# A new order of issue and new buffers for an adaLN, Hedgehog attention and MLP kernel on one core

## The chip, the cores and the metric

The kernel runs on one core of a Trainium2 chip. The metric is the device time of one execution in microseconds, as a median of runs. A profiled execution of the same kernel gives a page of figures and a trace; its span is a little shorter than the measured time. TensorE is PE in the profile (its weight loads PEld), VectorE is DVE, ScalarE is ACT, GpSimd is POOL, and SyncE is SP, whose queue issues nearly all the DMA transfers.

## The reference

One batch, S = 2048 tokens, D = 512, 32 heads of 16, a hidden width of F = 1376, all in fp32. Cut to what matters:

```python
mod = (silu(c) @ w_mod).reshape(1, 6, 1, -1)          # sa, ca, ga, sb, cb, gb
h = layernorm(x) * (1 + ca) + sa
q, k, v = heads(h @ wqkv)
pq, pk = q @ w_phi, k @ w_phi                         # per head, 16 x 16
phi_q = concat([softmax(pq), softmax(-pq)])           # 32 features per head
phi_k = concat([softmax(pk), softmax(-pk)])
kv = sum_s phi_k^T v ;  z = sum_s phi_k               # over all tokens, per head
o = (phi_q @ kv) / (phi_q . z + 1e-6)
x = x + ga * (o @ wo)
h = layernorm(x) * (1 + cb) + sb
x = x + gb * (gelu_tanh(h @ w1 + b1) @ w2 + b2)
```

The sum over all tokens in kv and z divides the work: nothing behind it can be finished before all keys and values are done.

## The kernel before

The work is tiled into eight blocks of 256 tokens (two tiles of 128). Products of full precision are made of three matmuls (`mm3`, line 287): each operand is split into a high and a low part, and high·high, high·low and low·high are added. A projection of one tile is thus a group of 12 matmuls of 128 rows by 512 columns; the rows "x12", "x24" of the chain are such groups.

The program has twelve parts. Part 0 loads, folds w_phi into the key and query weights (tiles `fold`), makes the modulation vectors and the layernorm of block 0 (`hT` is a block transposed). Parts 1 to 6 project keys, values and some queries (`pk`, `pv`, `pq` are PSUM banks), make the exponentials `ek`, and add up kv (`pkv`, a run of small matmuls in plain fp32). Part 7 closes the sums: `kvT` is copied by ScalarE, two small products `zp` and `kvp` follow, and `zb` is z spread over the partitions. It then does the attention of blocks 0 and 1, lays out w1 (`w1`, w2 as `w2a` and `w2b`), and starts on the MLP. Parts 8 to 11 run the MLP for pairs of blocks (`pg` is the hidden layer before and after the bias, `g` its GELU split in two, `py` the second product), with the attention of the later blocks threaded between.

Attention of a block (`attn_a`, line 742): with `eq` the exponentials of the queries of a tile, `ez` = eq·zb, `dz` its sum per head and sign, `den` the denominators, `rd` their reciprocal, `rcq` the factors of the rows, and last eq·rcq. In the two first blocks one of the two `ez` and one of the two last products go to VectorE, the rest to GpSimd; from block 2 on GpSimd has them all. Blocks 0 and 1 are then turned by TensorE (`qp`, `attn_t`, line 798, copies `qT`); in later blocks VectorE turns 32x32 pieces into `eb`, eight stores (`et_dram`) bring them to DRAM, and two loads bring them back as `eT` (`attn_ea`, line 779). `po` (`attn_o`, line 816) is the product with kv, copied into `oT` by ScalarE and VectorE, and `pw` the product with wo. `x1` is the residual; a second layernorm gives `h2`, `yp` its transposition by TensorE, and `yT` the result. Queries that are projected early are parked in DRAM: `qs` is the copy, `pq_dram` the store, `pq` the load.

The order is written out by hand, as data. `Held` and `Later` (lines 210 to 243) do not issue an operation but record it, in a queue by part and by "item.letter", where the letter is that of the engine (p, a, v, g, s for TensorE, ScalarE, VectorE, GpSimd, SyncE). `issue` then takes them out in the order of the twelve strings of `ISSUE` (line 87), one string for each part; a + or − in front of a name takes the operation from a later or an earlier part. One global sequence is thus cut into one queue for each engine, and each engine works through its own in order. All operations therefore have the line 218 in the profile. A framework sets the semaphores that the data and the buffers need.

Buffers are data too: `SLOTS` (line 46) has for each tag a string with one character for each allocation, which `slot` (line 258) reads. There are 19 large buffers ("buf"), 8 PSUM banks ("bank"), and two or three buffers for the small tags. Which earlier tile an allocation waits for follows from these characters.

## Time and profile before

| what | value |
|---|---|
| time, median of 3 runs | 467.59 us (467.13 to 468.8) |
| span of the profiled execution | 466.6 us, so 1.0 below the median |
| granted clock of TensorE | full speed in every slice |
| busy: PE, DVE, ACT, POOL | 458.5, 317.1, 234.6, 279.7 us |
| DMA moved | 68.05 MB, 146 GB/s on the mean |

The page gives each engine's busy time, its share of the span and its number of instructions, then the chain of work that ended last. A row of the chain or of a timeline is: start in us, length in us, engine, tile and line, and how many instructions; in square brackets the idle time before it and what ended that. A row of the waits is: who waited for whom, us in total, how often, the longest. In rows of groups, what stands after the bar is busy us, mean ns of one, and idle time before.

### The profile page before, as it was taken

The numbers are of one execution on the slowest core, as the hardware profiler recorded it, in microseconds if no ns is written. First come the engines' busy times: TensorE is split into PE (matmuls) and PEld (weight loads), VectorE is DVE, ScalarE is ACT, GpSimd is POOL, SyncE is SP. The second block draws the span as 40 slices with busy tenths as digits, with TensorE's granted clock in tenths as the row PEclk, the third lists the DMA queues.
The fourth block names the chain that finished last, engine by engine and source line by source line (L and its number), as shares of the span: only waits on it lengthen the run. The fifth ranks groups of instructions, "written<-read, shape, count | busy, mean of one in ns | idle before, by whom it ended". The sixth has DMA issues, their size and how long they took to land.

```text
span 466.6 us, 8536 instructions
## 1 busy us (share of the span) xinstructions
PE 458.5 (98%) x3297; PEld 372.3 (80%) x3297; DVE 317.1 (68%) x612; ACT 234.6 (50%) x381; POOL 279.7 (60%) x233
## 2 busy tenths in 40 slices
PE   8999999999999999999999999999999999999996
PEld 5887888888878878978787878787788788788884
DVE  5999999989938599389797579896484472221113
ACT  4757866767440827848537743176133234422221
POOL 2369587999799998989899684756721020300000
PEclk9999999999999999999999999999999999999999
DMA  8998738492372664836837728077445504000003
GB/s 311 382 311 301 195 84 276 95 269 55 100 257 95 189 209 90 244 104 139 224 135 160 225 53 241 1 130 178 143 90 136 122 14 93 15 30 1 1 1 135
DMA packets 83673, 68.05 MB, mean 146 GB/s; under 512 B 54688, under 2 KB 70960, under 8 KB 83376
## 3 DMA queue, kind: packets, MB, share of 16 engines
q1 hardware_dynamic: 83632, 67.50, 50.9%
q8 instruction: 26, 0.43, 0.4%
q14 instruction: 15, 0.12, 0.1%
HBM read 44.94 MB, written 22.55 MB: 145 GB/s over the span
## 4 chain that ended last, share of the span: by engine, by line
PE 85%; DMA 5%; DVE 4%; POOL 2%; issue 1%; ACT 1%; SPq 0%; DVEq 0%; POOLq 0%; ACTq 0%
PE py L218 25%; PE pg L218 24%; PE pv L218 8%; PE pk L218 8%; PE pw L218 8%; PE pq L218 7%; PE pkv L218 2%; DMA wm<-in_wmodT 2%; PE po L218 1%; DVE pw L218 1%; DMA eT<-et_dram 1%; DMA wms<-in_wmodT 1%; DMA xt<-in_x 1%; PE qp L218 1%; POOL w2a L218 1%
## 5 line engine op out<-in xcount | busy, mean ns | idle before, releaser
L218 PE MATMUL pg<-yT,w 128*128 128x512 f32 (+1 forms) x528 | 115.3, 371 | 0.6 <-DVE yT L218 0.3
L218 PEld LDWEIGHTS pg<-yT,w 128*128 128x128 f32 x528 | 92.8, 188 | 18.5 <-DVE yT L218 0.5
L218 ACT ACTIVATE pg<-pg,blob 128x512 f32<-128x512 f32 x44 | 29.1, 662 | 100.6 <-PE pg L218 100.4
L218 PE MATMUL py<-w2a,g 128*128 128x512 f32 x288 | 70.7, 391 | 0.0
L218 DVE TENSOR_TENSOR g<-pg,g 128x512 fp32r<-128x512 f32 x40 | 27.2, 680 | 61.7 <-ACT g L218 61.7
L218 PEld LDWEIGHTS py<-w2a,g 128*128 128x128 f32 x288 | 53.6, 188 | 12.6 <-issue 1.6
L218 PE MATMUL pk<-wk,hT 128*128 128x512 f32 x192 | 46.2, 392 | 0.8 <-ACT hT L218 0.7
L218 PE MATMUL py<-w2b,g 128*128 128x512 f32 x192 | 46.9, 391 | 0.0
L218 PE MATMUL pv<-wvh,hT 128*128 128x512 f32 x192 | 45.9, 392 | 0.0
L218 PE MATMUL pw<-wo,oT 128*128 128x512 f32 x192 | 45.4, 390 | 0.0
L218 PE MATMUL pq<-wq,hT 128*128 128x512 f32 x192 | 45.3, 391 | 0.0
L218 PEld LDWEIGHTS pk<-wk,hT 128*128 128x128 f32 x192 | 35.6, 188 | 9.1 <-ACT hT L218 1.1
L218 PEld LDWEIGHTS py<-w2b,g 128*128 128x128 f32 x192 | 35.9, 188 | 8.1 <-issue 0.7
L218 PEld LDWEIGHTS pw<-wo,oT 128*128 128x128 f32 x192 | 35.9, 188 | 7.8 <-issue 0.4
L218 PEld LDWEIGHTS pv<-wvh,hT 128*128 128x128 f32 x192 | 35.7, 188 | 7.5
L218 PEld LDWEIGHTS pq<-wq,hT 128*128 128x128 f32 x192 | 35.8, 188 | 7.3
L218 POOL TENSOR_TENSOR ez<-eq,zb 128x1024 f32<-128x1024 f32 x15 | 36.8, 2469 | 5.5 <-ACT last L218 3.0
L218 POOL TENSOR_TENSOR yT<-yf,yT 128x256 fp32r<-128x256 f32 x24 | 17.2, 742 | 35.1 <-ACT yT L218 35.0
L218 POOL TENSOR_TENSOR ek<-ek,rck 128x1024 f32<-128x1024 f32 x16 | 30.8, 1939 | 4.5 <-DVE rck L218 2.3
L218 POOL TENSOR_TENSOR eq<-eq,rcq 128x1024 f32<-128x1024 f32 x15 | 28.9, 1937 | 0.3
L218 ACT ACTIVATE g<-pg 128x512 fp32r<-128x512 f32 x40 | 24.0, 599 | 9.5 <-PE pg L218 4.4
L218 DVE TENSOR_REDUCE smq<-eq 128x64 f32<-128x1024 f32 x16 | 19.2, 1207 | 6.8 <-ACT eq L218 6.8
(153 smaller groups left out, 783.4 us busy)
## 6 DMA issues: line engine op xcount, KB each, us to landing
et_dram<-eb SPq DMA_DIRECT2D x48, 128.0 KB, 2.9
eT<-et_dram SPq DMA_DIRECT2D x12, 512.0 KB, 5.1
xt<-in_x SPq DMA_DIRECT2D x8, 512.0 KB, 6.1
wms<-in_wmodT SPq DMA_DIRECT2D x8, 512.0 KB, 5.9
x<-in_x SPq DMA_DIRECT2D x8, 512.0 KB, 5.2
out<-x SPq DMA_DIRECT2D x15, 256.0 KB, 2.5
nt_dram<-nb SPq DMA_DIRECT2D x28, 128.0 KB, 3.4
hd<-nt_dram SPq DMA_DIRECT2D x7, 512.0 KB, 5.5
```

What stands on the lines that cost most here:

```text
L218: return lambda *a, **k: self.later.hold(self.letter, lambda: f(*a, **k))
```

## The change

The operations stay the same, in kind and number; only the strings of `SLOTS` and `ISSUE` are others. That changes the order on all five engines, and which tiles share a buffer. The loads of ScalarE's function table, which the framework sets where the function changes, go from 16 to 12 by the new order. One row in each of the two tables, the rest is of the same kind:

```diff
 SLOTS = {
     "buf":
-    "e93cf0idhabf4g55a2h17e4i27ce25986gi96f88af4a115357h8gbbf584dec522e4g0bai8761904137ecd23b5bh77df6ae2i"
+    "21638bca4938165777cd2aadbic0357e91b8a566ih449254975e1ee816dfd239917i83fdc5ha9654g632bbh0ebi2681bgfe7"
...
 ISSUE = [
...
-q2.p a1.g a0.v +a0.v q0.p a0.v +a0.g a1.v a1.g a0.v q2.p q2.a -v0.v a0.g a1.v a0.g q0.p a0.g a0.v a1.g a1.g a0.g
+a1.v q2.p q0.p a0.g q0.p a0.g a0.g a0.v --bg.a +a0.a +a0.v +a0.g a1.g a1.g a1.g +a0.a q2.a a1.v q1.p a0.g a0.v q4.a
```

GpSimd's queue in part 7, from the denominators of block 0 to the last product of block 1 (`den_401`, `rcq_228`, `eq_391` are of block 0; `dz_415`, `den_432`, `rcq_262`, `eq_406`, `eq_407` of block 1; `ez_522`, `ez_523` of block 2). Before:

```order
L218 TENSOR_TENSOR den_401<-den_401,deps_109 128x64
L218 TENSOR_TENSOR dz_415<-dz_415,rcq_262 128x128
L218 TENSOR_TENSOR den_432<-dz_415 128x64
L218 TENSOR_TENSOR rcq_228<-rcq_228,rd_402 128x128
L218 TENSOR_TENSOR den_432<-den_432,deps_109 128x64
L218 TENSOR_TENSOR eq_391<-eq_391,rcq_228 128x1024
L218 TENSOR_TENSOR rcq_262<-rcq_262,rd_433 128x128
L218 TENSOR_TENSOR eq_406<-eq_406,rcq_262 128x1024
L218 TENSOR_TENSOR eq_407<-eq_407,rcq_262 128x1024
L218 TENSOR_TENSOR ez_522<-eq_514,zb_116 128x1024
```

Now:

```order
L218 TENSOR_TENSOR den_401<-den_401,deps_109 128x64
L218 TENSOR_TENSOR ez_522<-eq_514,zb_116 128x1024
L218 TENSOR_TENSOR dz_415<-dz_415,rcq_262 128x128
L218 TENSOR_TENSOR den_432<-dz_415 128x64
L218 TENSOR_TENSOR den_432<-den_432,deps_109 128x64
L218 TENSOR_TENSOR rcq_228<-rcq_228,rd_402 128x128
L218 TENSOR_TENSOR eq_391<-eq_391,rcq_228 128x1024
L218 TENSOR_TENSOR rcq_262<-rcq_262,rd_433 128x128
L218 TENSOR_TENSOR ez_523<-eq_515,zb_116 128x1024
L218 TENSOR_TENSOR eq_406<-eq_406,rcq_262 128x1024
L218 TENSOR_TENSOR eq_407<-eq_407,rcq_262 128x1024
```

The two multiplications of block 2 moved ahead of what the blocks 0 and 1 still need; and the last quarter of the exponentials of block 2 (eq from mxq and pq, 128x512), which stood between the second and the third ez of the blocks 0 and 1, moved ahead of all three. VectorE's part of the same work, ez_400 and eq_390 of block 0, stays in its place between them.

SyncE's queue at the transposes of block 2 (`et_dram_100`, its loads `eT`; `pq_dram_75` holds the parked queries of block 4, tile pq_620 is their load; the numbers here are those of the tiles in DRAM). Before:

```order
L218 DMA et_dram_100<-eb 32x16x64 x8
L218 DMA pq_dram_75<-qs 128x1024
L218 DMA eT<-et_dram_100 128x4x256
L218 DMA w1s<-in_w 128x4x128
L218 DMA ws<-in_w 128x1024
L218 DMA eT<-et_dram_100 128x4x256
L218 DMA pq<-pq_dram_75 128x1024
L218 DMA x_530<-in_x 128x2x512
```

Now:

```order
L218 DMA pq_dram_75<-qs 128x1024
L218 DMA pq<-pq_dram_75 128x1024
L218 DMA et_dram_100<-eb 32x16x64 x8
L218 DMA eT<-et_dram_100 128x4x256 x2
L218 DMA x_530<-in_x 128x2x512
```

The store and the load of the parked queries went ahead of the eight stores; two weight loads that stood between the loads of eT moved elsewhere.

The same queue at the transposes of block 5 (`et_dram_103`; `x_696` is the second load of x for block 5). Before:

```order
L218 DMA out<-x_451 128x512 x2
L218 DMA et_dram_103<-eb 32x16x64 x8
L218 DMA pq<-pq_dram_78 128x1024
L218 DMA x_696<-in_x 128x2x512
L218 DMA eT<-et_dram_103 128x4x256 x2
```

Now:

```order
L218 DMA out<-x_451 128x512 x2
L218 DMA et_dram_103<-eb 32x16x64
L218 DMA x_696<-in_x 128x2x512
L218 DMA et_dram_103<-eb 32x16x64 x7
L218 DMA eT<-et_dram_103 128x4x256 x2
```

The load of x moved from behind the eight stores to behind the first. Its buffer is also another: by the new string it is one from which TensorE still reads a hidden tile g in the second product of an earlier pair of blocks.

Elsewhere: the first x load stands ahead of the load of the constants; the first query projection ahead of two pieces of the key projection; the small matmuls of `pkv` run in nine runs, not six; a query projection stands between the last of them and `zp`; one stage of `yp` stands ahead of a query projection, not behind it.

## The prediction

> **What bounds the kernel now.** I read the page's busy shares first, then the waits of TensorE, then the chain of waits, and last the timelines of the places where the order changes.

> ```profile
> PE 458.5 (98%) x3297; PEld 372.3 (80%) x3297; DVE 317.1 (68%) x612; ACT 234.6 (50%) x381; POOL 279.7 (60%) x233
> PE 85%; DMA 5%; DVE 4%; POOL 2%; issue 1%; ACT 1%; SPq 0%; DVEq 0%; POOLq 0%; ACTq 0%
> ```

> TensorE is busy for 98% of the span and has 85% of the chain; no other engine passes 68%. The change neither adds nor removes a matmul, so it can only win or lose the little time in which TensorE waits. That time stands in its waits (total us, times, longest):

> ```profile
> PE fold L218 <- DMA k<-in_wkT: 0.9, 1, 0.9
> PE pk L218 <- ACT hT L218: 0.7, 1, 0.7
> PE zp L218 <- ACT kvT L218: 0.6, 1, 0.6
> PE pg L218 <- DVE yT L218: 0.3, 1, 0.3
> PE pg L218 <- ACT yT L218: 0.3, 1, 0.3
> PE po L218 <- DMA eT<-et_dram: 0.2, 1, 0.2
> PE pk L218 <- POOL hT L218: 0.2, 1, 0.2
> ```

> These are 3.2 us in all, 0.7% of the span: an upper bound for what better order can take away, beside some startup time before the first dense matmul. A loss has no such bound, since each new wait on TensorE is time in full. So I look for the places where the new order gives an operand later than TensorE asks for it. The chain shows the rhythm around the end of the k/v stage:

> ```profile
> 97.85 1.84 PE pkv L218 x142
> 99.69 2.95 PE pv L218 x12
> ...
> 133.35 1.79 PE pkv L218 x116
> ...
> 135.66 1.99 PE zp L218 x8
> ...
> 137.87 16.36 PE pq L218 x72
> 154.24 1.75 PE qp L218 x16
> 155.98 2.73 PE pq L218 x12
> 158.71 1.02 PE po L218 x32
> ```

> Twelve matmuls of 512 columns take 16.36/6 = 2.73 us; I count the distance between two points of TensorE's order in these units.

> **The sum, part by part.** All terms are against the profiled span of 466.6 us; the median of the runs, 467.59, is 1.0 above it, which I add at the end.

> *Startup.* The first x load now goes out ahead of the constants, and the first query projection ahead of two pieces of the key projection. The two pk waits above (0.7 and 0.2) may shrink, or the later of two half blocks comes in late by as much: −0.2, bounds −0.9 and +0.9, the sum of the same rows either way.

> *Entries into pkv.* After a run of pkv the next 12 matmuls took 2.95 and not 2.73, so each entry costs 0.22. The change cuts the pkv work into nine runs where there were six: +0.7, bounds +0.4 and +0.9 (some runs are shorter).

> *Other waits of the k/v stage.* One v projection now stands 0.6 us of work behind the copy that frees its bank; others have over 2 us. +0.2, bounds 0 and +1.5 (two such copies at the 0.7 of the pk row above).

> *kvT.* A query projection (2.73) now stands between the last pkv and the z matmuls, which covers the 0.6 of the zp row: −0.6. The bounds are −0.6 and 0.

> *The first two attention blocks: the largest term.* Here GpSimd and VectorE multiply 128x1024 tiles, and they get in each other's way:

> ```profile
> 138.61 4.78 POOL L218 TENSOR_TENSOR ez<-eq,zb 128x1024 f32<-128x1024 f32 x2
> 143.32 1.09 POOL L218 TENSOR_TENSOR eq<-mxq,pq 128x512 f32<-128x512 f32 x1
> 144.35 3.41 POOL L218 TENSOR_TENSOR ez<-eq,zb 128x1024 f32<-128x1024 f32 x1
> 147.83 0.46 POOL L218 TENSOR_TENSOR dz<-dz,rcq 128x128 f32<-128x128 f32 x1
> 148.37 0.29 POOL L218 TENSOR_TENSOR den<-dz 128x64 f32<-128x64 f32 x1
> ...
> 149.88 0.43 POOL L218 TENSOR_TENSOR rcq<-rcq,rd 128x128 f32<-128x128 f32 x1
> ...
> 150.52 1.94 POOL L218 TENSOR_TENSOR eq<-eq,rcq 128x1024 f32<-128x1024 f32 x1
> 152.41 1.42 POOL L218 TENSOR_TENSOR rcq<-rcq,rd 128x128 f32<-128x128 f32 x1
> ```

> ```profile
> 143.33 2.16 DVE L218 TENSOR_TENSOR ez<-eq,zb 128x1024 f32<-128x1024 f32 x1
> ...
> 151.06 2.48 DVE L218 TENSOR_TENSOR eq<-eq,rcq 128x1024 f32<-128x1024 f32 x1
> ```

> ```profile
> L218 DVE TENSOR_TENSOR wvh<-wv_s,wvh 128x1024 fp32r<-128x1024 f32 x1 | 1.2, 1208 | 0.0
> ```

> The same size takes VectorE 1.21 alone. Its ez took 2.16 and ended at 145.49, 1.08 behind the end of GpSimd's eq (144.41); its eq took 2.48 and ended at 153.54, 1.08 behind the end of GpSimd's (152.46). GpSimd's next ez took 3.41 instead of 4.78/2 = 2.39, its rcq 1.42 instead of 0.43. The one waits for the end of the other. [...]

> Let E be the end of zp_397 and Z the start of GpSimd's first ez. Before, Z was 138.61 and E 137.65 (135.66+1.99). Now the last pkv, which GpSimd's work ahead of it waits for, ends a query projection earlier, so GpSimd stands ready, and I take 0.76, what the copy into zb needs; the 1.09 of eq that stood between the ez is ahead of them. The two ez of GpSimd end at Z+4.8. VectorE's ez_400, ready at Z+3.6, waits for that and ends at 5.85; GpSimd's ez_422, begun at 4.8, is held as long and ends at 8.1. Then come dz and den (1.2) and, new here, ez_522 (2.39): 11.7. The second block's dz and den take to 12.8, rcq_228 to 13.25, eq_391 (1.94) to 15.2. VectorE's eq_390 is held until then and ends at 16.25. TensorE asks for it after 72 matmuls: E+16.36 = Z+15.6. Wait: 0.7. Before, it was ready at 153.54 for 154.24, so a margin of 0.7 turns into a wait. Next on GpSimd: rcq_262, held by eq_390 until 16.5, the second new one, ez_523, to 18.9, eq_406 to 20.85, eq_407 to 22.8. TensorE, begun on qp at 16.3, wants eq_407 after 1.75+2.73+1.02 = 5.5, at 21.8: wait 0.9. And VectorE's rd_525, which needs GpSimd's den_524 behind eq_407, stands ahead of the copy oT1_419 that the first pw group needs: 0.25. Sum +1.85, bounds +0.2 (no holding, below) and +2.8 (the held ones at 1.42−0.43 more).

> *yT.* One transposition stage (yp_479) is ahead of a query projection: it covers the two yT waits (−0.6) but its h2 is due 2.7 us sooner (+0.6). Net 0, bounds −0.6 and +0.6.

> *Transposes of block 2.* In SyncE's queue the load of pq_620, which waits for the landing of its own store, now stands ahead of the eight stores of et:

> ```profile
> 183.27 5.14 SPq L218 DMA_DIRECT2D et_dram<-eb  x8
> 188.51 0.48 SPq L218 DMA_DIRECT2D pq_dram<-qs  x1
> ```

> ```profile
> 193.29 6.65 DMA eT<-et_dram
> ```

> ```profile
> 184.93 0.59 ACT L218 ACTIVATE qs<-pq 128x512 f32<-128x512 f32 x1
> 186.07 1.09 ACT L218 ACTIVATE yT<-yp 128x512 fp32r<-128x512 f32 x2 [0.55 <-PE yp L218]
> ```

> ```profile
> 186.22 6.00 PE L218 MATMUL pg<-yT,w 128*128 128x256 f32 x48
> ```

> The landing times, shortest, median and longest, of the stores of et, the stores of pq and the loads of eT:

> ```profile
> DMA to landing us min/median/max: 2.2/2.9/7.1
> ```

> ```profile
> DMA to landing us min/median/max: 2.9/4.5/8.8
> ```

> ```profile
> DMA to landing us min/median/max: 3.7/5.1/7.1
> ```

> The store of pq waits for ScalarE's second qs, behind one yT (0.55) and a first qs, after the last yp: 0.55+0.59+0.59 and 0.3 of hand-overs = 2.05. Store to landing 3.4 (nearer the shortest, since SyncE has nothing else out), issue 0.4, eight stores 5.14, the last one's landing 2.9, eT_529 4.5 (below the median: the two weight loads that stood ahead of it, when it took 6.65, are gone). Sum 18.4. TensorE gets there after five half groups of pg (6.00/4 each, 7.5), one whole, 27 matmuls of py and 8 of po (0.6): 16.9. Wait 1.5 in place of 0.2: +1.3, bounds −0.2 (shortest landings: 16.0, no wait) and +4.5 (medians of the stores, and 6.65).

> *Block 3 and its yf.* The same chain has 12.1 of work for some 12.2: +0.1, bounds 0 and +1.

> *Block 5.* The load x_696 waits for TensorE's end of a py group (its buffer holds the g read there) and now stands behind the first of the eight et stores, not behind them all:

> ```profile
> 276.94 5.20 SPq L218 DMA_DIRECT2D et_dram<-eb  x8
> 282.24 0.47 SPq L218 DMA_DIRECT2D pq<-pq_dram  x1
> 282.82 0.53 SPq L218 DMA_DIRECT2D x<-in_x  x1
> ```

> Behind that py: x 0.53, seven stores 7×0.65 = 4.55, landing 2.9, issue 0.4, eT 4.3 (between shortest and median) = 12.7. TensorE gets there after four whole groups and half of po, 4×2.73+0.5 = 11.4. A wait up to 1.3; a part lies behind what SyncE would wait for anyway, so I take +0.8, bounds 0 (shortest: 11.4) and +2.1 (median load, 0.8 more).

> *From block 6 to the end.* The waits that move there end at least 0.4 us before TensorE asks, and in the tail nothing moves: 0, bounds 0 and +1.

> Sum: −0.2+0.7+0.2−0.6+1.85+0+1.3+0.1+0.8 = +4.15, a span of 470.75, and with the 1.0: **471.8 us**, 0.9% over 467.59.

> **Rivals.**
> 1. *Faster.* The search covers the waits and opens none, and the entries cost their lower bound: 466.6−3.2+0.4+1.0 = 464.8. For it: the zp and yT covers are real, and GpSimd has 40% idle. Against it: the startup waits hang on loads that both orders begin with. Chance 0.16.
> 2. *No change.* VectorE and GpSimd do not hold each other, so ez_422 ends at 7.15, eq_390 at 13.5 and eq_407 at 20.8, ahead of 15.6 and 21.1, and the transfers land at their shortest: the term of attention falls to 0.2, both eT terms to 0. 471.8−1.65−1.3−0.8−0.1 = 468.0. For it: the shortest landings occur. Against it: the twofold 1.08. With only the one or the other true it goes up to 469.9. Chance 0.29.
> 3. *Slower by more.* SyncE's queue decides: its round trip of store and load before the et stores takes the medians. With the price of 4.5 in place of 1.3: 475.0; it decides from 16.9 on, the moment at which TensorE asks. For it: the 6.65. Against it: fewer loads are out at once. Chance 0.12.

> **How the numbers follow.** The forecast has 0.43, its own range 470.0 to 473.4 (each of the three large terms half-way to its bounds, not all together). The range, 466.0 to 474.6, leaves out half of the first rival and half of the third. A measurement of this kernel tells about 0.5% from no change, 2.3 us: 465.3 to 469.9. Faster by more holds most of the first rival, 0.12; same 0.33 (the second, and the rest of the first); slower 0.55 (forecast and third).

> **What would show it.** In the profile of the changed kernel: the zp wait on kvT gone; TensorE waiting 0.5 to 1 us twice in qp for eq, with VectorE's eq ending some 1.1 behind GpSimd's; po waiting about 1.5 us for the eT of block 2 and up to 1.3 for that of block 5; and no other wait above 0.5 behind 36 us. It is wrong if TensorE's waits still sum to about 3 us, or if a wait stands at a place not named here.

## The result and the profile after

| | before | after |
|---|---|---|
| time, median of 4 runs each | 467.62 us | 488.31 us (486.01 to 492.55) |
| ratio, with its 95% interval | 1 | 1.045 (1.0399 to 1.0501) |
| span of the profiled execution | 466.6 us | 484.2 us |
| granted clock in that execution | full | full |

The changed kernel, called after from here on, is 20.7 us slower than the kernel before; 471.8 was forecast, with a range to 474.6. The direction was right, the size was not: the profiled execution alone lost 17.6 us where the sum had 4.15. Of the other 3.1 us, 2.3 stand between the profiled execution of after (486.01) and the median: in its other three executions the mean clock was 0.993 to 0.996, which is one or two stretches of 3.4 us at half clock, of which more below. The rest is that the profiled execution of before lay above its own median (466.6 and the 1.8 that lie between span and time in after make 468.4).

The page of after, busy time and chain:

```profile
PE 464.1 (96%) x3297; PEld 370.4 (77%) x3297; DVE 321.1 (66%) x612; ACT 229.9 (47%) x377; POOL 280.7 (58%) x233
PE 52%; DMA 15%; POOL 10%; DVE 7%; ACT 6%; issue 5%; SPq 3%; DVEq 0%; POOLq 0%; ACTq 0%
```

TensorE does the same 3297 matmuls, but only 52% of the chain is its own where it was 85%. The waits of TensorE (total us, times, longest):

```profile
PE po L218 <- DMA eT<-et_dram: 3.6, 4, 1.5
PE pkv L218 <- issue: 1.8, 1, 1.8
PE py L218 <- DVE g L218: 1.7, 1, 1.7
PE pv L218 <- POOL wvh L218: 1.5, 1, 1.5
PE pk L218 <- ACT qs L218: 1.4, 1, 1.4
PE pv L218 <- POOL hT L218: 1.1, 1, 1.1
PE qp L218 <- POOL eq L218: 1.0, 2, 0.6
```

No single wait is large; all rows of this view, 19 waits, sum to 16.0 us, against 8 waits and 4.1 us before. To place them I worked out a **delay** from each trace: the matmul work of TensorE is added up at full rate, and at the same amount of work done one reads by how much TensorE is behind that. All stage figures below are worked out in this way; where a stage is cut shifts a figure by a few tenths. Its growth against the kernel before, stage by stage, in us:

| stage (us of matmul work) | predicted | measured |
|---|---|---|
| start (0 to 52) | −0.2 | +4.4 |
| rest of the k/v stage, entries into `pkv` among it (52 to 126) | +0.9 | +2.0 |
| inside the last run of `pkv` (126 to 128) | – | +2.1 |
| `kvT` (128 to 148) | −0.6 | −0.6 |
| attention of blocks 0 and 1 (148 to 160) | +1.85 | +1.8 |
| `yT` (160 to 175) | 0 | +0.2 |
| transposes of block 2 (175 to 207) | +1.3 | +0.4 |
| block 3 (207 to 240) | +0.1 | +2.0 |
| `py` behind `g` (240 to 246) | – | +2.0 |
| to the end of block 5 (246 to 296) | +0.8 | +1.2 |
| block 6 (296 to 320) | 0 | +1.8 |
| to the end | 0 | +0.4 |
| sum | +4.15 | +17.7 |

**The start.** SyncE's queue, before:

```profile
15.99 0.33 SPq L218 DMA_DIRECT2D nt_dram<-nb  x1
16.91 1.98 SPq L218 DMA_DIRECT2D nt_dram<-nb  x3
23.87 0.38 SPq L218 DMA_DIRECT2D hd<-nt_dram  x1
```

and after:

```profile
10.83 0.33 SPq L218 DMA_DIRECT2D wv_s<-in_wv  x1
17.65 0.33 SPq L218 DMA_DIRECT2D nt_dram<-nb  x1
18.08 0.44 SPq L218 DMA_DIRECT2D xt<-in_x  x1
18.57 1.01 SPq L218 DMA_DIRECT2D nt_dram<-nb  x2
19.63 1.78 SPq L218 DMA_DIRECT2D wv_s<-in_wv  x1
21.45 1.72 SPq L218 DMA_DIRECT2D nt_dram<-nb  x1
27.43 0.38 SPq L218 DMA_DIRECT2D hd<-nt_dram  x1
```

The queue issues nothing between the load at 10.83 and 17.65: at its head stands the first store of nb, the transposed layernorm. VectorE's row of the second transpose, before and after:

```profile
15.26 0.70 DVE L218 STREAM_TRANSPOSE nb<-xt 128x512 f32<-128x512 f32 x1
```

```profile
16.92 0.70 DVE L218 STREAM_TRANSPOSE nb<-xt 128x512 f32<-128x512 f32 x1
```

It is 1.7 later. The first one could not start before 14.75, since products `fold` still read its new buffer until 14.30 (until 11.1 before), and the second stands some operations behind it. Everything behind the head of the queue shifts: the load back, hd, goes out 3.6 later, and the load of wv_s that stands among the stores makes wvh late (the 1.5).

**The last run of pkv.** TensorE, and the window in which it stops (the columns of the second are the busy us of PE, PEld, DVE, ACT and POOL with counts, the granted clock, the DMA share and GB/s):

```profile
135.74 2.45 PE L218 MATMUL pkv<-ek,vf 128*17 128x32 f32 x245
140.03 0.88 PE L218 MATMUL pkv<-ek,vf 128*17 128x32 f32 x75 [1.84 <-issue]
```

```profile
138.00:140.00 2.00, 0.19 (x21) 0.08 (x9) 0.00 (x0) 0.00 (x0) 1.26 (x2) 1.00 0.81 220
```

TensorE stops in the middle of a row of equal matmuls and waits for nothing that the profile names. The page has a DMA queue for instructions:

```profile
q8 instruction: 26, 0.43, 0.4%
```

These are 26 fetches with 0.43 MB, 16 KB each. TensorE has 6644 records in this trace (matmuls, weight loads and their semaphores), so a fetch is worth some 256 of its instructions, an estimate from these two counts. One fetch was under way here: it began at 137.77 and landed at 138.91, and TensorE went on at 140.03, with 3009 instructions behind it.

**Attention of blocks 0 and 1.** GpSimd, one row of VectorE, then TensorE:

```profile
146.49 4.77 POOL L218 TENSOR_TENSOR ez<-eq,zb 128x1024 f32<-128x1024 f32 x2 [0.66 <-ACT zb L218]
155.74 2.39 POOL L218 TENSOR_TENSOR ez<-eq,zb 128x1024 f32<-128x1024 f32 x1
159.75 3.00 POOL L218 TENSOR_TENSOR eq<-eq,rcq 128x1024 f32<-128x1024 f32 x1
165.43 3.83 POOL L218 TENSOR_TENSOR eq<-eq,rcq 128x1024 f32<-128x1024 f32 x2
```

```profile
159.79 1.16 DVE L218 TENSOR_TENSOR eq<-eq,rcq 128x1024 f32<-128x1024 f32 x1
```

```profile
162.80 1.89 PE L218 MATMUL qp<-blob,eq 128*128 128x128 f32 x15 [0.46 <-POOL eq L218]
169.32 1.86 PE L218 MATMUL qp<-blob,eq 128*128 128x128 f32 x15 [0.56 <-POOL eq L218]
```

In time this is the forecast nearly to the tenth. With Z = 146.49, the start of GpSimd's first ez, eq_407 was to be ready at Z+22.8; it ended at 169.26, Z+22.8. But who holds whom at the second meeting turned round: VectorE's eq_390, which starts 0.04 behind, runs its 1.16 and ends 1.80 ahead, and GpSimd's eq_391 takes 3.00 instead of 1.94.

**Block 3, and py.** TensorE in block 3; then VectorE and TensorE at g_614:

```profile
226.13 0.66 PE L218 MATMUL po<-eT,gab 64*32 64x256 f32 x16
228.32 0.67 PE L218 MATMUL po<-eT,gab 64*32 64x256 f32 x16 [1.52 <-DMA eT<-et_dram]
```

```profile
264.35 0.71 DVE L218 STREAM_TRANSPOSE eb<-eq 128x512 f32<-128x512 f32 x1 [2.46 <-DMA yt_dram<-yb]
264.98 0.65 DVE L218 TENSOR_TENSOR g<-pg,g 128x512 fp32r<-128x512 f32 x1
```

```profile
265.69 2.56 PE L218 MATMUL py<-w2b,g 128*128 128x512 f32 x10 [1.73 <-DVE g L218]
```

The po of block 3 stands 11 us of work earlier in TensorE's new order, and its transfers do not come as much sooner. At g_614, VectorE's queue has at its head a transpose whose buffer, by the new string of buffers, is still being stored as yb; g stands behind it, and TensorE waits for g. A comparison of orders alone doesn't show this one: it comes from a buffer and a queue together.

**Block 6.** SyncE, and TensorE:

```profile
331.85 0.38 SPq L218 DMA_DIRECT2D yf<-yt_dram  x1
332.28 1.68 SPq L218 DMA_DIRECT2D et_dram<-eb  x2
334.06 4.19 SPq L218 DMA_DIRECT2D eT<-et_dram  x2
```

```profile
341.85 0.67 PE L218 MATMUL po<-eT,gab 64*32 64x256 f32 x16 [1.21 <-DMA eT<-et_dram]
```

The load yf_676 now stands ahead of the last two stores that eT waits for. It does not wait itself, but while it is on its way those two stores land 5.1 and 4.3 us after their issue, the six ahead of them after 2.6 to 3.1; the second load of eT waits for them.

### The profile page after: what moved, and what is told of

It is laid out like the page before. It is cut to its first block, busy times and chain, and to the rows that moved or that the text cites. A ratio compares the mean times of both kernels' runs of the same rounds, so it can differ in the third digit from the quotient of the medians.

```text
span 484.2 us, 8598 instructions
## 1 busy us (share of the span) xinstructions
PE 464.1 (96%) x3297; PEld 370.4 (77%) x3297; DVE 321.1 (66%) x612; ACT 229.9 (47%) x377; POOL 280.7 (58%) x233
## 4 chain that ended last, share of the span: by engine, by line
PE 52%; DMA 15%; POOL 10%; DVE 7%; ACT 6%; issue 5%; SPq 3%; DVEq 0%; POOLq 0%; ACTq 0%
PE pg L218 18%; PE py L218 17%; PE pv L218 5%; PE pw L218 4%; SPq L218 3%; PE pk L218 3%; POOL ez L218 3%; DMA eT<-et_dram 3%; POOL eq L218 2%; DMA et_dram<-eb 2%; DMA hd<-nt_dram 2%; PE pq L218 2%; DMA wm<-in_wmodT 2%; DMA nt_dram<-nb 2%; PE pkv L218 1%
## 5 line engine op out<-in xcount | busy, mean ns | idle before, releaser
L218 PE MATMUL pg<-yT,w 128*128 128x512 f32 (+1 forms) x528 | 114.0, 371 | 0.5 <-DVE veb L218 0.5
L218 PEld LDWEIGHTS pg<-yT,w 128*128 128x128 f32 x528 | 92.3, 188 | 18.8 <-DVE veb L218 0.9
L218 ACT ACTIVATE pg<-pg,blob 128x512 f32<-128x512 f32 x44 | 29.1, 661 | 96.1 <-PE pg L218 95.9
L218 PE MATMUL py<-w2a,g 128*128 128x512 f32 x288 | 69.2, 391 | 0.0
L218 DVE TENSOR_TENSOR g<-pg,g 128x512 fp32r<-128x512 f32 x40 | 27.1, 684 | 60.7 <-ACT g L218 60.7
L218 PEld LDWEIGHTS py<-w2a,g 128*128 128x128 f32 x288 | 53.5, 188 | 13.1 <-issue 2.1
L218 PE MATMUL pv<-wvh,hT 128*128 128x512 f32 x192 | 46.8, 396 | 2.8 <-POOL wvh L218 1.5
L218 PE MATMUL py<-w2b,g 128*128 128x512 f32 x192 | 47.0, 392 | 1.7 <-DVE g L218 1.7
L218 PE MATMUL pk<-wk,hT 128*128 128x512 f32 x192 | 46.6, 394 | 1.4 <-ACT qs L218 1.4
L218 PE MATMUL pw<-wo,oT 128*128 128x512 f32 x192 | 45.7, 391 | 0.0
L218 PE MATMUL pq<-wq,hT 128*128 128x512 f32 x192 | 45.6, 392 | 0.0
L218 PEld LDWEIGHTS pv<-wvh,hT 128*128 128x128 f32 x192 | 35.2, 188 | 11.7 <-POOL wvh L218 1.9
L218 PEld LDWEIGHTS py<-w2b,g 128*128 128x128 f32 x192 | 35.7, 188 | 10.5 <-DVE g L218 2.2
L218 PEld LDWEIGHTS pk<-wk,hT 128*128 128x128 f32 x192 | 35.4, 188 | 9.9 <-ACT qs L218 1.8
L218 PEld LDWEIGHTS pw<-wo,oT 128*128 128x128 f32 x192 | 35.8, 188 | 8.2 <-issue 0.4
L218 PEld LDWEIGHTS pq<-wq,hT 128*128 128x128 f32 x192 | 35.7, 188 | 7.5 <-ACT zb L218 0.2
L218 POOL TENSOR_TENSOR ez<-eq,zb 128x1024 f32<-128x1024 f32 x15 | 36.6, 2460 | 2.0 <-PE py L218 1.0
L218 POOL TENSOR_TENSOR rsc<-vec,mhalf 128x1 f32<-128x1 f32 x16 | 8.8, 550 | 40.9 <-DVE vec L218 40.9
L218 POOL TENSOR_TENSOR ek<-ek,rck 128x1024 f32<-128x1024 f32 x16 | 30.9, 1948 | 1.6 <-DVE rck L218 1.4
L218 POOL TENSOR_TENSOR eq<-eq,rcq 128x1024 f32<-128x1024 f32 x15 | 30.0, 2011 | 0.4
L218 POOL TENSOR_TENSOR yT<-yf,yT 128x256 fp32r<-128x256 f32 x24 | 17.0, 740 | 15.2 <-ACT yT L218 15.2
L218 ACT ACTIVATE g<-pg 128x512 fp32r<-128x512 f32 x40 | 24.0, 599 | 1.6
```

What stands on the lines that cost most here:

```text
L218: return lambda *a, **k: self.later.hold(self.letter, lambda: f(*a, **k))
```

## The experiments

Times are single executions, beside 467.7 to 468.4 us for the kernel before on the same chip, unless an interval is given. "Delay" is that of the table above, over the kernel before. In the diffs, a row is one operation in the queue of the engine named.

Two stages must be read with their spread. In the eight traces of after and of experiments on it that leave the start alone, the delay of the start was 2.5 to 4.6 (median 3.8), so a single trace does not settle a difference of 1 us there. The growth from 240 to 246, at g_614, was 1.5 to 2.4 wherever it wasn't edited, and that in block 6 1.0 to 2.1, where no half-clock stretch fell into it.

### The stop in pkv

**e1.** After, with two groups of the last run put into the run ahead of it: 192 and 192 matmuls in place of 64 and 320.

```diff
 TensorE
 pkv <- ek_329
+pkv <- ek_331
+pkv <- ek_357
 pv (last value projection)
-pkv <- ek_331
-pkv <- ek_357
 pkv <- the rest
```

> The changed kernel with two of the five groups of pkv at the end of the k/v stage (ek_331, ek_357) moved ahead of the last value projection, so that the run of 160 small matmuls (320 records) becomes 96 and 96. Theory (the instruction stream): in the changed kernel TensorE stops for 1.84 us with nothing to wait for, just after 245 records, while a 16 KB fetch in the queue of instructions is on its way; small matmuls of 10 ns use up the stream faster than fetches of 0.9 to 1.4 us bring it. Then the stop is gone and TensorE's delay behind its full-rate work falls by 1.8 to 2.1 us at zp. Rival (data): something unseen holds group ek_374; then the stop stays, at the same group, at 1.5 us or more.

Measured: 487.75, and two stops where the theory had none:

```profile
135.89 2.35 PE L214 MATMUL pv<-wvh,hT 128*128 128x512 f32 x9 [1.74 <-issue]
140.92 0.88 PE L214 MATMUL pkv<-ek,vf 128*17 128x32 f32 x74 [1.51 <-issue]
```

```profile
139.00:140.00 1.00, 0.41 (x49) 0.29 (x33) 0.00 (x0) 0.00 (x0) 0.00 (x0) 1.00 0.00 0
```

They stand behind the 2753rd and the 3009th instruction of TensorE, 256 apart, by the estimate above the size of one fetch. The second begins while no data moves at all (DMA share 0.00). So in e1 a stop came without data traffic, and the places of both go by the count of instructions. That suggested the block theory of e5: TensorE runs dry of instructions where it works through a block of 256 of them sooner than the next fetch comes.

**e2.** The kernel before, with its last run lengthened by the group ek_357, to 256.

```diff
 TensorE
-pkv <- ek_357
 pv, pq
+pkv <- ek_357
 pkv <- the last run
```

> The kernel before with one group of pkv (ek_357) moved to the head of its last run, which grows from 96 to 128 small matmuls (192 to 256 records); the run it leaves shrinks from 64 to 32. Theory of the instruction stream: 256 records are just above the 245 at which the changed kernel stopped, so a stop of 0.3 to 1.5 us comes within the run or at its end, and the kernel gets slower by that. Rival (data): no stop, change below 0.3 us.

Measured: 473.14. No stop of this kind, but another wait:

```profile
PE pkv L215 <- POOL ek L215: 3.7, 2, 2.6
```

GpSimd's first operation into eq_514 takes the buffer of ek_357 next and stands ahead of ek_374 in its queue, so pkv waits for itself by way of GpSimd: delay +4.75. TensorE thus spent 3.9 us on the block of 256 that ends at the 3009th instruction, and the question of e2 stays unanswered; what it shows is that one group, moved behind three projections, costs more than the whole forecast.

**e5.** After, with the query projection pq_404, which stood behind the run, put into it: 192, then pq, then 128.

```diff
 TensorE
 pkv (192)
+pq_404
 pkv <- ek_374 and the rest (128)
-pq_404
 zp
```

> The changed kernel with the query projection pq_404, which stands behind the last run of pkv, moved into it, ahead of the group of ek_374: the run of 160 becomes 96 and 64. In the changed kernel and three variants of it the stops lay at the TensorE instructions 2753 and 3009 of the trace (matmuls and weight loads counted together), which are 256 apart, the content of one 16 KB fetch. Theory (a block of small matmuls): a stop comes where a whole block of 256 instructions is pkv and so lasts 1.3 us, less than the 3 us from one block's start to the next one's arrival; with 12 large matmuls (2.7 us) in the block that ends at 3009 no stop over 0.4 us stays, although the run ahead of it still has 96. The wait of zp for kvT comes back with 0.5 to 0.7, so TensorE's delay between 52 and 132 us of work falls by 1.2 to 1.6. Rival (length of the run): a run of 96 stops here as in the first experiment, over 1.2 us.

Measured: 484.37. The stop is gone (the delay does not grow inside the run), which agrees with the block theory. But the 0.6 of kvT is back, and the waits of qp for eq grow from 1.0 to 2.0. From 126 to 160 us of work, the end of attention, the delay grows by 3.3 in e5 as in after: what the stop gave is taken back whole. GpSimd's work starts behind the last pkv, which now ends directly ahead of zp, and it sets when eq is ready. In after this wait lies partly under the stop.

### The start

**e3.** After, with the loads wv_s_142 and wms_170 ahead of the first store of nb in SyncE's queue.

```diff
 SyncE
+wv_s_142 <- in_wv
+wms_170 <- in_wmodT
 nt_dram <- nb (first store)
 xt_238 <- in_x
 nt_dram <- nb x2
-wv_s_142 <- in_wv
 nt_dram <- nb
 xt
-wms_170 <- in_wmodT
```

> The changed kernel with two loads (the second half of wv_s, and wms_170) moved in SyncE's queue ahead of the first store of nb, which waits for VectorE's transposes until 17.6 us. Theory (the queue): SyncE stood from 10.8 to 17.6 behind that store while the transfers in flight ran out, about 3 us of the start's transfer time were lost, and all four startup waits of TensorE (wvh 1.6, hT 1.3, qs 1.5, wms 1.0) come from that. Then wvh's wait goes (below 0.3) and TensorE's delay at 52 us of work falls from 7.5 by 2 to 4 us. Rival (order of engines): only wvh's wait goes, 1.6 us, and the three others stay, since they come from the order in which GpSimd and ScalarE take the modulation columns; then the delay falls by 1.3 to 1.9.

Measured: 490.0. The wait for wvh is gone, but wms_170 waits for its own buffer and goes out at 19.50, ahead of the stores; the delay at the start is 5.2. Both expectations missed.

**e6.** After, with wv_s_142 ahead of the first store and xt_238 behind all four.

```diff
 SyncE
+wv_s_142 <- in_wv
 nt_dram <- nb (first store)
-xt_238 <- in_x
 nt_dram <- nb x2
-wv_s_142 <- in_wv
 nt_dram <- nb
+xt_238 <- in_x
```

> The changed kernel with two loads moved at the start of SyncE's queue: the second half of wv_s ahead of the first store of nb (its buffer is free from 12 us on, unlike that of wms_170, which held the queue up in the earlier attempt), and xt_238 from among the four stores to behind them. Theory (the queue): the stores then land some 2 to 3 us sooner, hd_164 is issued by 24.5 instead of 27.4, the wait for wvh goes (below 0.3), and the sum of TensorE's delay at 52 us of work comes out at 3.5 to 5.3 (7.5 in the changed kernel, 6.3 and 6.4 in two variants with the same start). Rival (order of engines: GpSimd and ScalarE take the modulation columns first): the wait for wvh goes, the others stay, and the delay stays at 6 or more.

Measured: 484.58. The delay at the start falls to 1.2, outside the spread. The kernels below that have these moves too scatter: 2.8, 2.4 and 1.8 in e15, e17 and e18, which move a transpose as well, but 4.0 and 3.1 in e10 and e12, which move an operation of GpSimd. The place of the two loads is a part of the loss; how large a part is not settled (2.6 in e6, against the median of 3.8). And little of it arrives at the end (+16.3 against +17.7). In e6 the stop in pkv is followed by something that the profiled run of after does not have:

```profile
137.00:139.00 2.00, 1.58 (x78) 1.38 (x78) 0.00 (x0) 0.59 (x2) 0.54 (x1) 0.92 1.01 377
139.00:141.00 2.00, 2.00 (x6) 1.52 (x5) 0.00 (x0) 0.74 (x1) 1.71 (x2) 0.50 1.06 374
```

TensorE is granted half its clock (the column with 0.50) for one stretch of 3.4 us.

**e10.** As e6, with the multiplication into wms_195 (the text on record calls it an addition) behind the second half of hT1_184 in GpSimd's queue.

```diff
 GpSimd (beside the moves of e6)
-wms_195 *= cb
 hT1_184 (second half)
+wms_195 *= cb
```

> The changed kernel with the two moved loads of the start experiment, and on GpSimd the second half of hT1_184, which TensorE needs, ahead of the addition to wms_195, which waits for its load. Theory (queued behind a foreign wait): the wait of pv for hT (0.8 in the start experiment) goes, TensorE's delay at 52 us of work falls from 4.3 to 3.0 to 3.7. Rival: the modulation columns are the bound, so the wait comes back at pc or pk, and the delay stays at 4.0 or more.

Measured: 489.67. The wait for hT goes, and ScalarE, whose copy vf stands behind wms_195, is late instead:

```profile
PE pk L215 <- ACT vf L215: 2.2, 1, 2.2
```

Delay at the start +4.0, the rival's side.

**e14.** After, with VectorE's second transpose of nb_163 behind the first.

```diff
 VectorE
 nb_163 <- xt (first)
+nb_163 <- xt (second)
 ... (hp, prod, affine, hT)
-nb_163 <- xt (second)
```

> After, with VectorE's second transpose of nb_163 (the one that ended at 17.62) put directly behind the first one in VectorE's queue; no load is moved. Theory: VectorE's place in the order is half of the loss at the start; SyncE's stores of nt stand behind that transpose, so they and the load hd_164 land 1 to 1.5 sooner, and the delay of TensorE after the start (4.4 more than before, at 52 us of its work) falls by 1 to 2.5, to 2 to 3.4. Rival: the load xt_238, whose buffer comes free only at 16.2, holds the queue anyway, and the wait for wvh (whose load stands behind the stores) stays: the delay falls by less than 0.7.

Measured: 485.36; the delay at the start is 2.6, which the theory had, but 2.5 occurs without any edit there, and e15 and e17, with both kinds of edit, are not ahead of e6. Moved up, the second transpose waits for ScalarE's half of xt and starts at 16.21, 0.7 sooner than in after, and the first store goes out at 16.95. That the late transpose makes its part of the loss is what the queue shows, and not settled by this run.

**e11 and e16.** The kernel before, with its load wv_s_141 ahead of the first store and xt_238 behind that store; first one execution (e11), later twelve (e16).

```diff
 SyncE
+wv_s_141 <- in_wv
 nt_dram <- nb (first store)
+xt_238 <- in_x
-wv_s_141 <- in_wv
 nt_dram <- nb x3
-xt_238 <- in_x
```

> The kernel before, with one part of the change alone: at the start of SyncE's queue the first half of wv_s ahead of the first store of nb, and the load xt_238 from ahead of that store to behind it, as the change has it. Theory (this order of loads carries the loss of the start): hd_164 is issued 2 us later or more than at 23.9, and TensorE's delay at 52 us of work rises from 3.1 by 1.5 to 4. Rival (the loss comes from the order on VectorE, GpSimd and ScalarE): it rises by less than 0.5.

> The kernel before with its load of wv_s_141 ahead of the first store of nb and xt_238 behind it, as in the single look that ended at 467.48 against 467.82; now with an interval. Theory: it wins the 0.9 us of delay that its trace showed, ratio 0.998 (0.9965 to 0.9995). Rival: the difference is that of one execution; ratio 1.000 with 1 inside the interval.

Measured: 467.48 beside 467.82; then 468.04 beside 467.74, ratio 1.0004 (0.9993 to 1.0014). Moving xt_238 among the stores is one of the things that the change does, and in the kernel before it costs nothing; that this is because the transposes are early there is likely, but not tested. The 0.9 us of delay that e11 won was that of one execution, and no better kernel comes of it.

### Attention of blocks 0 and 1

**e7.** After, with the two new multiplications of GpSimd behind eq_407 again. VectorE's queue, with the sums of them, stays in its order.

```diff
 GpSimd
 den_401
-ez_522 <- eq_514
 dz_415
 ...
-ez_523 <- eq_515
 eq_406, eq_407
+ez_522 <- eq_514
+ez_523 <- eq_515
```

> The changed kernel with GpSimd's ez_522 and ez_523 (and VectorE's two sums of them) moved behind eq_407, where they stood before the change. Theory (the prediction's): the two waits of qp for eq (0.6 and 0.8 with hand-overs) go, eq_407 ends 4.5 to 5 us sooner counted from the first ez, and TensorE's delay between 132 and 160 us of work grows by 0.6 or less (2.3 in the changed kernel). Rival: the waits stay at 1 us or more, since GpSimd and VectorE hold each other whatever the order.

Measured: 493.69. The first wait of qp for eq is gone and its delay with it (0.1 instead of 0.8 there), so the ez in front were its cause; behind it stands a new and larger one:

```profile
174.54 2.82 PE L215 MATMUL qp<-blob,eq 128*128 128x128 f32 x12 [3.06 <-ACT qs L215]
```

The copy qs_403 takes the buffer of ez_523 next. In the new string of buffers the moved multiplications are needed early, to free what follows: order and buffers hang together, and here the one could not be undone without the other.

### Queues behind the transposes

**e4.** After, with two edits: g_614 ahead of the transpose eb_642 on VectorE, and the last two stores of block 6 ahead of yf_676 on SyncE.

```diff
 VectorE
+g_614 <- pg_613
 eb_642
-g_614 <- pg_613
 SyncE
+et_dram <- eb_757 (last two)
 yf_676 <- yt_dram
-et_dram <- eb_757 (last two)
```

> The changed kernel with two moves far apart: on VectorE g_614, which TensorE waits for, ahead of the transpose eb_642, which waits for the landing of stores; on SyncE the last two stores of et of block 6 ahead of the load of yf_676, which stood among them. Theory (queued behind a foreign wait): the wait py for g (1.9 us at 265) falls below 0.4, that of po for eT_759 (1.5 us at 342) below 0.5, and the total falls by 2.5 to 3.5 us. Rival (the transfers themselves are late): both waits move to the next user of the same data, and the total falls by less than 1 us.

Measured: 483.05, span 481.2. VectorE's g now ends at 260.74, not at 265.63, and the 1.7 of py goes:

```profile
260.09 0.65 DVE L215 TENSOR_TENSOR g<-pg,g 128x512 fp32r<-128x512 f32 x1
```

Between 240 and 246 us of work the delay grows by 0.7 instead of 2.0, and by 0.7 again in e12 and e17, which have this edit too: the cause is shown. In block 6 it grows by 0.9 instead of 1.8, by 0.6 in e12 and 1.4 in e17, against the 1.0 to 2.1 without the edit: the direction is likely, the size is not shown. The two stores now land 2.8 and 3.3 us after their issue, but the loads of eT take 5.8 and 5.3, where they took 5.2 and 3.9. By the end the delay is 2.9 less, of which 1.1 is the start, where nothing was edited.

**e8.** After, with the load pq_620 behind the two loads of eT of block 2, and in block 3 a piece of w1 on GpSimd behind den_575 and the reciprocal rd_576 ahead of g_518 on VectorE. The reciprocal is thus taken ahead of the last addition to den_575, so this part of the computation (the small constant in these denominators) is left out; the same holds for e9 and e12.

```diff
 SyncE
-pq_620 <- pq_dram
 et_dram <- eb x8
 eT x2
+pq_620 <- pq_dram
 GpSimd
-w1_377
 den_575
+w1_377
 VectorE
+rd_576
 g_518
-rd_576
```

> The changed kernel with three moves at the transposes of blocks 2 and 3: the load of pq_620 behind both loads of eT of block 2; on GpSimd the last piece of w1 behind the denominators of block 3; on VectorE rd_576 ahead of g_518. Theory (queues): the wait of po for eT_529 (0.9) falls below 0.3, that for eT_580 (1.8) below 0.6, the total falls by 2 to 2.6. Rival (SyncE's rate: 8 stores take 5 us to issue, and the loads of eT another 4.4): the second wait stays at 1.2 or more, since the stores of eb_578 are bound by the landing of eT_529, whose buffer they take.

Measured: 491.8. VectorE's maximum over pq_620 stands in its queue where the order expected the load, so it now waits there, and the g behind it come late: pw waits 1.8 for g, and block 3 loses more than it did (delay 12.3 at block 2's end, 18.9 behind block 3, a half-clock stretch among it: the mean clock of this execution was 0.993). Missed.

**e9.** Only the edits of block 3 from e8.

```diff
 GpSimd
-w1_377
 den_575
+w1_377
 VectorE
+rd_576
 g_518
-rd_576
```

> The changed kernel with two of the three moves of the experiment on the blocks 2 and 3: the last piece of w1 on GpSimd behind the denominators of block 3, rd_576 on VectorE ahead of g_518; the load of pq_620 stays where the change put it. In that experiment VectorE stood at a maximum over pq_620 until its load came and everything behind it was late. Theory (queues): without that move the products of block 3 end 1.2 to 1.5 us sooner, and the wait of po for eT_580 falls from 1.8 to 0.3 to 0.7; eT_529 keeps its 0.9. Rival: rd_576 waits for GpSimd and now holds up the g behind it, so a new wait of py, pg or pw for g of 0.8 or more appears, and nothing is won.

Measured: 487.87, and po's waits for eT are 4.2 instead of 3.6. Missed: neither e8 nor e9 brought the transfers forward far enough.

**e13.** After, with small groups of py put ahead of po on TensorE: the other way round, po asks later.

```diff
 TensorE
+py (1 group)
 po of block 2
-py (1 group)
+py (4 groups)
 po of block 3
-py (4 groups)
 ... (2 groups at block 5, 4 at block 6)
```

> After, with small groups of py put ahead of the po groups in TensorE's queue: one ahead of po_535 of block 2, four ahead of the po of block 3, two ahead of the po of block 5, four ahead of the po of block 6; nothing else. Theory: the changed order asks for the turned queries too early (block 3's po 11 us of TensorE's work sooner than before), so the waits of po for eT (3.6 us in four places) and of py for g behind them are only a matter of what stands ahead: eT falls to 1.0 or less, the total by 2.5 to 4, to 484 to 486. Rival: the py groups then want a g that VectorE has not yet made, or the pw behind them comes late: a new wait of py on g or of pw, total within 1 us of after.

Measured: 487.57, ratio 1.0422 (1.0401 to 1.0443). The waits now:

```profile
PE pw L215 <- ACT oT L215: 1.9, 1, 1.9
PE py L215 <- DVE g L215: 1.4, 1, 1.4
...
PE po L215 <- DMA eT<-et_dram: 0.2, 1, 0.2
```

The first half of the theory is shown: po's 3.6 come from TensorE asking too early, and 0.2 are left. The second half falls: nothing is won. In block 6 the pw behind po comes sooner after it, and ScalarE has a function table and an exponential between the two copies oT:

```profile
347.42 3.18 PE L215 MATMUL pw<-wo,oT 128*128 128x512 f32 x8 [1.89 <-ACT oT L215]
```

A half-clock stretch follows that wait too (granted clock 0.50 from 349 to 352). The delay is 14.9 ahead of it, where after has 17.3, and 18.9 behind it.

### All together

**e12.** After, with the moves of e5, e8 (without pq_620), e4 and e10.

```diff
 SyncE, GpSimd: as e10
 TensorE: as e5
 GpSimd, VectorE: as e9
 VectorE, SyncE: as e4
```

> The changed kernel with all moves that were to undo a loss: the two loads and hT1_184 at the start, pq_404 in the run of pkv, g_614 ahead of eb_642, the two stores ahead of yf_676, and the two moves of block 3. Theory (independent waits, each worth what its place showed): some 3 to 4 us at the start, 1.9, 1.5 and 1.3 at the three later places, 0 to 1 at pkv, and no halved clock since no stop of 2 us is left: 476 to 480 us, 1.018 to 1.027 of the kernel before. Rival (the waits hang together: what one sets free, the next loses): 483 or more.

Measured: 486.39, ratio 1.0388 (1.0348 to 1.0429).

**e15.** After, with only moves that had taken a wait away: e6, e14, the g_614 of e4, and e13. The text on record also names the last two stores of block 6; the kernel that ran does not have that move.

```diff
 SyncE: as e6
 VectorE: as e14, and g_614 as in e4
 TensorE: as e13
```

> After, with the moves that won by themselves, together: the two load moves at the start (wv_s_142 ahead of the first store, xt_238 behind the four), the early transpose of nb_163, g_614 ahead of eb_642, the last two stores of block 6 ahead of yf_676, and the py groups ahead of the po groups. Theory: the waits are separate, so the gains add up: start 3.2 or more, g and yf 3, eT 2.5, together 8 to 10 of the 17.6 us, 478 to 480. Rival, by the joint run before: the waits hang together and each gain is met by a new wait or by a stretch of half clock; 483 or more. No theory expects it to fall under the kernel before.

Measured: 485.42, ratio 1.0355 (1.0319 to 1.0391), the rival's side. The delay ahead of the last run of pkv is 4.9 against 6.4 in after; behind it, it is 10.5 against 8.6:

```profile
140.77 0.97 PE L215 MATMUL pkv<-ek,vf 128*17 128x32 f32 x75 [4.13 <-issue]
```

```profile
137.00:139.00 2.00, 0.00 (x0) 0.00 (x0) 0.00 (x0) 0.00 (x0) 0.72 (x1) 1.00 0.96 309
141.00:143.00 2.00, 2.00 (x73) 1.72 (x67) 0.00 (x0) 1.16 (x2) 1.06 (x1) 0.59 0.54 179
```

The stop (4.13) is twice as long, and half clock follows it: from 126 to 160 the delay grows by 7.2 where after has 3.3.

**e17.** The sum once more, now without the stop: e6, e14, e4, the py groups of e13 for blocks 2, 3 and 5, and e5.

```diff
 SyncE: as e6 and e4
 VectorE: as e14 and e4
 TensorE: as e13 (not in block 6), and as e5
```

> After, with the moves of the joint run (start loads, early transpose of nb_163, g_614 ahead of eb_642, py groups ahead of the po of blocks 2, 3 and 5), the last two stores of block 6 ahead of yf_676 in place of the py groups there, and the query projection pq_404 put into the last run of pkv, which took the stop away before. Theory: the joint run lost its gains in the stop of TensorE in that run (delay 4.9 before it, 10.5 behind it); without the stop the delay behind pkv is at most 6, and with 1.4 given back in the qp waits and 0.6 in kvT, and 3 to 4 from block 2 to the end, the total is 11 to 13.5 over before: 478.5 to 481.5. Rival: what the stop cost is given back whole, since GpSimd's work behind the last pkv sets when eq is ready; 483.5 or more, with qp waits of 3 or more.

Measured: 483.14, ratio 1.0336 (1.0277 to 1.0396); delay at the end of the profiled execution 14.9. It falls between the two expectations. Inside pkv nothing is lost (6.1 before, 6.1 behind), as the theory had it. But from 126 to 160 the delay grows by 3.4, just as in after and in e5:

```profile
162.50 1.89 PE L215 MATMUL qp<-blob,eq 128*128 128x128 f32 x15 [1.44 <-POOL eq L215]
```

That sentence of the rival is right, though not its numbers. In after the stop takes nothing that GpSimd would not take; in e15 it took the gains, being longer and with half clock behind it. The intervals of e15 and e17 lie just below that of after (1.0399 to 1.0501); those of e12 and e13 overlap it.

**e18.** The kernel of e15, with the load w1s_386, issued as the stop begins, behind the load of eq_391.

```diff
 SyncE
-w1s_386 <- in_w1
 eq_406, eq_391 <- e_dram
+w1s_386 <- in_w1
 eq_407 <- e_dram
```

> The joint run's kernel (all moves with the py groups ahead of po), with the load w1s_386, which SyncE issues as the stop of TensorE in pkv begins, put behind the loads of eq that follow it. Theory: the stop is the wait for a fetch of instructions, and it is long (4.1 there, 2.1 in after) where the transfers of data already fill the DMA engines; with 512 KB less in front, some 1.3 us at the 400 GB/s of that stretch, the stop is 2.3 to 3.1. Rival: the fetch does not queue behind these transfers; the stop stays within 0.4 of 4.1, or of 2.1 if the 4.1 was that of one execution.

Measured: 487.84, a stop of 3.3, between the two expectations. The test was not clean either: the loads of eq moved up into the place of w1s and fill the DMA engines as much (share 1.09):

```profile
137.00:138.00 1.00, 0.00 (x0) 0.00 (x0) 0.00 (x0) 0.00 (x0) 0.00 (x0) 1.00 1.09 415
```

Whether the length of the stop comes from the data traffic stays open. The queue of instructions shows what goes with it: in the three long stops (3.3 in e3 and e18, 4.1 in e15) the fetch began 0.9 to 1.7 us after TensorE had stopped, in the eleven shorter ones 0.4 to 1.1 us before. Why it began late is not shown.

## Why the prediction came out as it did

**What bounds, and the sign: right.** The prediction argued that TensorE has almost nothing to gain and that each new wait is time in full. That is what happened; more than half of the chances lay on slower. What failed is the list of places: most of the loss stands where the sum had nothing or almost nothing. Its own last sentence had named that, a wait at a place not named, as the sign of being wrong.

**Attention, +1.85: right, by its mechanism.** The times from Z on came to the tenth, both waits of qp (0.6 and 0.8 with the hand-over, 0.46 and 0.56 as the profile counts them) stand where they were named, and e7 removed the first one by undoing its cause. The two engines held each other again. At their first meeting VectorE's ez_400 took 2.27 and ended 1.08 behind the end of GpSimd's ez (151.26), as twice before. At the second the prediction has VectorE's eq_390 held until GpSimd's eq_391 ends; here the one held was GpSimd's (3.00 against 1.94), although it begins 0.04 sooner. Which of two is held was the author's reading of the rows of before, and no run shows a rule for it. The second rival, no change without that holding, is excluded by these rows. Two details did not come: VectorE's eq was to end 1.1 behind GpSimd's and ended 1.80 ahead, which leaves the later end where it was, and the 0.25 at the first pw has no wait in the view. So the agreement to 0.05 is partly luck. e5 and e17 add that in after a part of this chain lies hidden under the stop.

**kvT, −0.6, and yT, 0: right.** The zp wait on kvT is gone; e5 and e17 brought it back (0.6, at kvp) by undoing the cover. yT came to +0.2.

**Entries into pkv and other k/v waits, +0.9: too small, +2.0.** The count of nine runs was right. An entry cost 0.15 to 0.32, so the three more make 0.5 to 1.0 of the 2.0; of the rest the view shows one wait of 0.2 (pv for vf), and what remains is not placed.

**Transposes of block 2, +1.3: too large, +0.4.** The round trip of pq was on SyncE's queue as described, but its store landed in 2.6, not in the 3.4 taken. The prediction also misread two of its rows: 2.9/4.5/8.8 and 2.2/2.9/7.1 mix stores with the loads back. The six stores of pq alone have 2.9, 3.8 and 8.8, the 48 of et 2.2, 2.9 and 3.8, so the upper bound of this term and the 475.0 of the third rival were some 0.7 too high.

**Startup, −0.2: the step that failed most, +4.4.** The bounds, −0.9 and +0.9, were those of two waits that the kernel before happened to show. The step counted what moves in TensorE's queue there; it did not count the stores of nb at the head of SyncE's queue, nor that VectorE's transpose, which releases them, had been given another buffer. e6 supports the part of the loads, in a spread as wide as its effect; that of the transpose is read from the queue, and e14 did not settle it. How the 4.4 divide stays open.

**Block 3, +0.1: failed, +2.0.** "The same chain has 12.1 of work for some 12.2" did not take in how far po itself had moved: it stands 11 us of work earlier now. e13 shows that this makes the wait.

**"From block 6 to the end: 0" and nothing for py: failed, +1.8 and +2.0.** Each comes from one row queued in front of what TensorE needs: eb_642, which waits for its buffer, shown by e4, and yf_676, beside which the last stores land late, where e4 supports only the direction. The sentence that the waits there end at least 0.4 ahead of TensorE's asking was read for the operands that moved, not for what was queued in front of them.

**The stop in pkv, +2.1: not foreseen at all.** The prediction had a price for a run of pkv only by its entry, and none for its length.

**Block 5, +0.8: about right in size at its place.** The stage grew by 1.2, of which 0.5 to 0.8, by where one cuts, stand at that block's po; the view has 0.25 there as a wait for eT. The rest is not placed.

The terms of the order that failed have one form. The orders were compared at the places that had a wait before or a visible move; most of the loss came at places that had none. TensorE waited 8 times before and 19 times after, for 4.1 and 16.0 us. The rival "slower by SyncE's queue", 475.0, had the right engine for two of the terms, at other places. And the undoing shows a second thing that a sum of terms does not have: what was won ahead of a stage was often lost in it. For the end of pkv and attention the runs show why: GpSimd's work behind the last pkv, and the clock. Elsewhere it was not traced.

## What to carry to other kernels

When a change permutes everything, do not bound it by the waits that the old profile shows. For each engine list the head of its queue at the times when the tight operands are due, with the buffer that this head waits for; this advice is drawn from the losses here and was not tried as a forecast. Order and buffers are tied: of the edits of after that have an interval none came below 1.0336 (e17), and a piece moved back by itself (e7) ran 5.4 us above the median of after, in one execution. A queue that does little is not free: at the start SyncE's issued nothing for 6.5 us behind one store that waited, and in block 6 one load put in front of two stores went with 1.8 us of delay.

## What of the hardware was not expected

**A stop for instructions.** In after, in the eleven experiments on it that keep the long run of pkv, and in e1, TensorE stops behind its 3009th instruction, in e1 also behind the 2753rd, for 1.5 to 4.1 us; it does not in the kernel before, nor where a projection stands inside the run (e5, e12, e17). A pkv matmul and its weight load are issued every 10 ns (245 in 2.45 us), so 256 instructions pass in 1.3 us. In each of the 14 stops a fetch that took 0.9 to 1.7 us landed, and TensorE went on 1.1 to 1.6 us after that. Runs of 192 alone do not decide it: e1 stops with them, the kernel before does not. Counted in blocks of 256 up to the 3009th, no block of before has over 231 instructions of pkv, and the shortest took it 3.8 us; the block that ends at the stop has 254 in after, which passed in 1.4 us. That the fetch is the cause is the likeliest reading of this; it was not tested by moving a fetch. Why some fetches begin late stays open.
